# Expert 0's weight pieces later in the attention stage: three at the beginning, the others behind the second step

## The chip, the cores and the metric

One core of one Trainium2 chip runs the whole program. The metric is the device time of one execution, in microseconds. The kernel before took 2313.67 us (median of three runs, 2310.92 to 2315.62).

The engines are named as in the profile: PE is TensorE's matmul, PEld its weight load, DVE is VectorE, ACT is ScalarE, POOL is GpSimd, SP is SyncE, which issues the DMAs. Each works through its own queue in order.

## The reference

Three computations follow one another, all in float32. A decay attention over 4 batches of 8 heads, 768 positions of width 48; a mixture over 8 experts of all 3072 tokens, with gate weights balanced by eight rounds of normalization; a bilinear layer.

```python
f = 1.0 / (1.0 + np.exp(-f_logit))
for t in range(S):
    state = f[:, :, t, :, None] * state + np.einsum('bhd,bhe->bhde', k[:, :, t], v[:, :, t])
    y[:, :, t] = np.einsum('bhd,bhde->bhe', q[:, :, t], state)
...
P = np.exp(logits)                      # logits = x @ w_gate, less their maximum
for _ in range(8):
    P /= P.sum(1, keepdims=True) + 1e-09
    P /= P.sum(0, keepdims=True) + 1e-09
    P *= N / E
for e in range(E):
    h = np.maximum(x @ w1[e], 0.0)
    out += P[:, e:e + 1] * (h @ w2[e])
...
return (x @ w_a) * (x @ w_b) @ w_out
```

## The kernel before

The program has two parts with a plan of instructions each. The first holds attention, the first half of the normalization rounds, all of expert 0, and preparations for the second. The second holds experts 1 to 7 and the bilinear layer; the change leaves its rules alone.

Attention goes in 24 steps of 128 positions (`attention(s)`, lines 362 to 595): a step loads f, q, k and v, transposes them on TensorE, computes decays on ScalarE and VectorE (lines 395 to 413), forms scaled copies of q and k (419 to 460), masked products (m0, m8, m16, m32, lines 435 to 500), the state, and y (line 576). Its x goes through a DMA that rearranges it (line 584, tile xf), is split into a high and a low part (lines 593, 594), and is also stored (line 589). Products in this kernel use three matmuls: high by high, high by low, low by high.

Expert 0 (`expert0(b)`, line 612) works on pairs of steps as "fill": the planner gives its matmuls a share of TensorE's time beside attention. Its first product is with wi0 and wi1 (4 blocks each of h, line 624), its second with wo0 and wo1 (line 642). The splits of h are GpSimd's (line 631).

Expert 0's weights are prepared in 14 pieces (`add_piece`, line 243): for each half u three pieces wi of 128 x 512 and four wo of 128 x 384. A piece is loaded into one of two buffers raw (line 250; a piece of wi is two DMAs), copied to its high part by ScalarE (line 233), and GpSimd subtracts that from the raw value for the low part (line 235). A buffer is free for the next piece when GpSimd is done. The main stage's first weight preparation (`w1_prep(plan, 1000 * 12, 0)`, line 775) loads 128 x 256 blocks into the tile stage (line 731), forms five differences on GpSimd, copies them on ScalarE and subtracts on GpSimd; as instructions of the plan these have line 778 in the profile.

What sets the order is a list scheduler (`Plan.order`, line 82). It keeps a modelled time for each engine, and at each turn takes, of the operations whose dependencies are done on that engine, the one with the lowest priority number. An operation with a low number comes early, but one with a high number is taken too as soon as its engine has nothing better. Dependencies are keys, strings that an operation reads or writes in the plan. The planner's times only choose the order; on the chip, an instruction waits for the tiles that it really reads or writes.

Of the kernel before, what the change touches and what calls it, by code (L numbers as in the profile page):

```python
# [40 lines left out]
def f32(ap):  # L41
    return ap.bitcast(F32)
# [90 lines left out]
def kernel(  # L133
# [22 lines left out]
    KD = DM // 128  # L156
# [5 lines left out]
    FU = 512  # L162
    FT = FU // 128
# [4 lines left out]
    LATE = 4.0  # L168
# [27 lines left out]
    wd = [spill.tile(list(sh), F32, name=f"wd{n}") for n, sh in enumerate(  # L196
        ((DM, DFF2), (DM, DFF2), (DFF2, DM)))] if wide else [w_a, w_b, w_out]
# [28 lines left out]
    def take_raw(m):  # L226
        n = count["raw"] % len(raws)
        count["raw"] += 1
        return f"raw{n}", raws[n][:, :m]

    def split_ops(plan, prio, got, gk, hj, lj, key, m):

        plan.add(prio, "ACT", .11 + m * .00107, [gk], [key], lambda: nc.scalar.activation(  # L233
            out=hj, in_=got, func=AF.Copy))
        plan.add(prio + 1, "POOL", .1 + m * .0026, [gk, key], [key], lambda: nc.gpsimd.tensor_tensor(  # L235
            out=lj, in0=got, in1=f32(hj), op=ALU.subtract))

    def moe_rows(e, c, m):

        src = w1[e, :, c:c + m].rearrange(ROWS, **ROWS_N)  # L240
        return [[(64 * hd, 64, src[kk, hd]) for hd in range(2)] for kk in range(KD)]

    def add_piece(plan, prio, key, parts, hj, lj, reads=()):

        m = hj.shape[-1]
        rk, raw = take_raw(m)

        def get():
            for p0, n, src in parts:
                nc.sync.dma_start(out=raw[p0:p0 + n], in_=src.bitcast(I32))  # L250

        plan.add(prio, "SP", .05 + m * .0013, reads, [rk], get, LATE)
        split_ops(plan, prio + 9, f32(raw), rk, hj, lj, key, m)
# [73 lines left out]
    PE, DVE, ACT, POOL, SP = "PE", "DVE", "ACT", "POOL", "SP"  # L327
    plan = Plan()
    used = {"T": 0, "O": 0, "M": 0}

    def gate():
# [8 lines left out]
        out=wgs[:, :, E:], in0=wg, in1=f32(wgs[:, :, 0:E]), op=ALU.subtract))  # L340
# [256 lines left out]
    def logits(s, prio):  # L597
        xH, xL = (x[:, :, (s % 2) * 128:(s % 2) * 128 + 128] for x in b_x[(s // 2) % 2])

        def lg(ps):  # L600
            n = 2 * KD
            for i in range(n):
                a, m = ((xH, 2 * E), (xL, E))[i % 2]
                nc.tensor.matmul(
                    out=ps[:, :m], lhsT=a[:, i // 2, :], rhs=wgs[:, i // 2, :m], start=(i == 0), stop=(i == n - 1))

        kl, psl = take("O", p_O)
        plan.add(prio, PE, .54, [f"x{s % 4}", "wgs"], [kl], lambda: lg(psl))
        plan.add(prio, DVE, .08, [kl], [f"lg{s}"], lambda: nc.vector.tensor_reduce(
            out=logit[:, s, :], in_=psl[:, :2 * E].rearrange("p (two e) -> p e two", two=2), axis=AX.X, op=ALU.add))  # L610
# [36 lines left out]
            op(SP, .55, [ky], [], lambda ys=ys, tt=tt: nc.sync.dma_start(  # L647
                out=y0[b * (EB // 128) + tt], in_=ys), 3.0)

    for u in range(2):  # L650
        (ih, il), (oh, ol) = w_e0[u]
        rows = moe_rows(0, u * FU, FU)
        for n in range(KD):
            add_piece(plan, 1000 + 120 * (7 * u + n), f"e0i{u}{n}", rows[n], ih[:, n], il[:, n])
        for n in range(FT):
            f0 = u * FU + n * 128
            add_piece(plan, 1000 + 120 * (7 * u + KD + n), f"e0o{u}{n}", [(0, 128, w2[0, f0:f0 + 128, :])],
                      oh[:, n], ol[:, n])

    def sinkhorn(plan, prio, lo, hi, nm, bufs):  # L660

# [37 lines left out]

    for i in range(NSTEP):  # L700
        attention(i)
        if i:
            logits(i - 1, 1000 * i + 500)
        if i % 2 == 1:
            expert0(i // 2)
    logits(NSTEP - 1, 1000 * NSTEP)
    sinkhorn(plan, 1000 * NSTEP, 0, ROUNDS1, "T", p_T)
    phases = [("moe", 0), ("moe", 1), ("out", 0), ("moe", 2), ("out", 1), ("out", 2)]
# [10 lines left out]
    def w1_prep(plan, prio, n):  # L719

        ph, _, _, e, c = jobs[n]
        if phases[ph][0] == "moe":
            parts = moe_rows(e, c, PW)
        else:
            parts = [[(0, 128, wd[e][kk * 128:kk * 128 + 128, c:c + PW])] for kk in range(KD)]
        j = n % 2
        st, (wh, wl) = stage[j], w1s[j]
        for kk, slot in W_RAW:
            def get(kk=kk, slot=slot):
                for p0, m, src in parts[kk]:  # L730
                    nc.sync.dma_start(out=st[p0:p0 + m, slot:slot + 2, :].rearrange("p s f -> p (s f)"), in_=src)

            plan.add(prio, SP, .38, [] if phases[ph][0] == "moe" else [f"wd{e}"], [f"sg{j}{kk}"], get, LATE)
        sk = [f"sg{j}{kk}" for kk in range(KD)]
        for o, a, b in W_SUMS:
            plan.add(prio + 1, POOL, .5, sk, [f"sg{j}s"], partial(
                nc.gpsimd.tensor_tensor, out=st[:, o], in0=st[:, a], in1=st[:, b], op=ALU.subtract))
        for x in range(2):
            s = slice(5 * x, 5 * x + 5)
            key = f"w1{n % 2}{x}"  # L740
            plan.add(prio + 600, ACT, .74, sk + [f"sg{j}s"], [key], partial(
                nc.scalar.activation, out=wh[:, s], in_=st[:, s], func=AF.Copy))
            plan.add(prio + 601, POOL, 1.75, sk + [f"sg{j}s", key], [key], partial(
                nc.gpsimd.tensor_tensor, out=wl[:, s], in0=st[:, s], in1=f32(wh[:, s]), op=ALU.subtract))
# [21 lines left out]
    prio = 1000 * 12  # L766
    ab = [(f"xr{n}", b_xr[n]) for n in range(2)]
    for blk, z, i in ((1, 0, 0), (3, 1, 2), (None, 0, 1), (0, 0, 4), (4, 0, 8), (1, 1, None), (4, 0, 6), (0, 0, 5),
# [4 lines left out]
        if i is not None:  # L773
            x_sum(plan, prio, i, ab if len(X_OF[i]) > 1 else [], ab[z], POOL)
    w1_prep(plan, 1000 * 12, 0)
    with tc.manual_schedule():
        for fn in plan.order(SHARE):
# [7 lines left out]
    plan = Plan()  # L785
# [149 lines left out]
    if wide:  # L935
        for n, (r, c, m) in enumerate(((DM, DFF2, 256), (DM, DFF2, 256), (DFF2, DM, 192))):
            later += [(n, r0, c0, m) for c0 in range(0, c, m) for r0 in range(0, r, 128)]
    w1_prep(plan, -2000, 1)
    hs, ws = [], []
    for n, (ph, u, f, e, c) in enumerate(jobs):  # L940
# [37 lines left out]
        if n + 2 < len(jobs):  # L978
            w1_prep(plan, 1000 * (n + 1) - 500, n + 2)
# [48 lines left out]
```

## Time and profile before

| | |
|---|---|
| median of 3 runs | 2313.67 us |
| profiled execution | 2310.98 us |
| span of its trace | 2309.2 us |
| PE busy | 2235.4 us (97%) |
| DVE busy | 1457.6 us (63%) |
| ACT busy | 1045.5 us (45%) |
| POOL busy | 1089.9 us (47%) |

The shares are means over the whole program. The first part, with attention, lies within the first 495 us; the rows further below cut it in two stages. "Busy" of an engine is the time in which it had an instruction at work, stretched instructions included.

### The profile page before, as it was taken

To read this page: it belongs to the slowest core of one execution; us is meant where nothing else is said; L and a number is where in the kernel's file an instruction comes from. 1 tells how busy PE (TensorE), PEld (TensorE's weight loads), DVE (VectorE), ACT (ScalarE), POOL (GpSimd) and SP (SyncE) were. 2 spreads that over 40 slices of the span, in tenths; PEclk is the share of its full clock that TensorE was granted. 3 is DMA by queue.
4 is the path that set the end of the run, shared out by engine and by line. 5 is a ranking of instruction groups with operands and counts; after the bars stand their busy time and mean duration, and the time that the engine had idled before them with its cause. 6 is when DMAs were issued, how large, how long until landed. Compare 5 with 4: busy or idle time off the path is not lost.

```text
span 2309.2 us, 41089 instructions
## 1 busy us (share of the span) xinstructions
PE 2235.4 (97%) x15523; PEld 2010.4 (87%) x15523; DVE 1457.6 (63%) x2572; ACT 1045.5 (45%) x1988; POOL 1089.9 (47%) x1231
## 2 busy tenths in 40 slices
PE   5998999999999999999999999999999999999999
PEld 4887888888999999889999998888999999988888
DVE  7889787657766775576666544565444444455644
ACT  3555555535434444534434444554434444444442
POOL 4113212147544445554545456665444444475661
PEclk9999999999999999999999999999999999999999
DMA  6445433233232332332222223123111111221210
GB/s 125 104 94 117 97 84 83 51 113 85 82 93 86 85 89 70 108 90 81 76 78 76 56 64 94 48 76 103 43 54 50 54 49 42 82 76 44 80 49 28
DMA packets 278263, 176.67 MB, mean 77 GB/s; under 512 B 146608, under 2 KB 267696, under 8 KB 278064
## 3 DMA queue, kind: packets, MB, share of 16 engines
q1 hardware_dynamic: 278064, 174.04, 28.4%
q8 instruction: 122, 2.00, 0.4%
q14 instruction: 77, 0.63, 0.1%
HBM read 143.27 MB, written 25.95 MB: 73 GB/s over the span
## 4 chain that ended last, share of the span: by engine, by line
PE 79%; DVE 14%; ACT 2%; SPq 2%; issue 1%; DMA 1%; POOL 0%; DVEq 0%; ACTq 0%; POOLq 0%
PE pF L845 37%; PE pR L275 35%; PE pM L275 2%; PE pM L263 2%; DVE fi L413 2%; DVE z L987 2%; DVE gl L987 2%; DVE X L470 1%; SPq L584 1%; DMA xf<-q 1%; PE pO L569 1%; DVE X L519 1%; DVE fi L407 1%; DVE fi L405 1%; DVE q L456 1%
## 5 line engine op out<-in xcount | busy, mean ns | idle before, releaser
L275 PE MATMUL pR<-w2h,gl 128*128 128x384 f32 x1632 | 550.4, 337 | 5.4 <-DVE gl L987 5.4
L275 PE MATMUL pR<-w2l,gh 128*128 128x384 f32 x1632 | 551.1, 338 | 0.0
L275 PE MATMUL pR<-w2h,gh 128*128 128x384 f32 x1632 | 547.9, 336 | 0.6 <-DVE sk_c L693 0.6
L987 POOL TENSOR_TENSOR w1l<-stage,w1h 128x640 fp32r<-128x640 f32 x238 | 386.4, 1626 | 328.9 <-ACT w1h L987 317.2
L845 PE MATMUL pF<-xsh,w1h 128*128 128x512 f32 x1320 | 516.6, 391 | 10.1 <-ACT z L987 5.1
L845 PE MATMUL pF<-xsh,w1l 128*128 128x512 f32 x1320 | 523.7, 397 | 1.4 <-POOL w1l L987 1.4
L845 PE MATMUL pF<-xsl,w1h 128*128 128x512 f32 x1320 | 521.8, 395 | 0.0
L987 DVE TENSOR_TENSOR z<-pF,z 128x512 f32<-128x512 f32 x378 | 259.9, 689 | 356.8 <-PE pF L845 317.0
L987 POOL TENSOR_TENSOR stage<-stage 128x128 f32<-128x128 f32 x595 | 298.6, 517 | 376.9 <-DMA stage<-in_moe_w_dram 318.4
L987 ACT ACTIVATE gh<-z 128x512 fp32r<-128x512 f32 x324 | 203.9, 631 | 395.3 <-DVE z L987 388.9
L987 ACT ACTIVATE z<-pF 128x512 f32<-128x512 f32 x378 | 225.3, 597 | 294.0 <-PE pF L845 283.6
L275 PEld LDWEIGHTS pR<-w2l,gh 128*128 128x128 f32 x1632 | 306.1, 188 | 31.4
L275 PEld LDWEIGHTS pR<-w2h,gh 128*128 128x128 f32 x1632 | 306.6, 188 | 30.6 <-DVE sk_c L693 0.9
L987 DVE SCALAR_TENSOR_TENSOR acc<-pR,prob,acc 128x384 f32<-128x384 f32 x336 | 206.2, 614 | 201.0 <-PE pR L275 200.0
L275 PEld LDWEIGHTS pR<-w2h,gl 128*128 128x128 f32 x1632 | 306.4, 188 | 7.9 <-DVE gl L987 7.9
L845 PEld LDWEIGHTS pF<-xsh,w1l 128*128 128x128 f32 x1320 | 247.6, 188 | 55.0 <-POOL w1l L987 1.9
L845 PEld LDWEIGHTS pF<-xsh,w1h 128*128 128x128 f32 x1320 | 248.1, 188 | 46.1 <-ACT z L987 10.1
L235 POOL TENSOR_TENSOR w2l<-raw,w2h 128x384 fp32r<-128x384 f32 x204 | 233.7, 1156 | 99.4 <-ACT w2h L233 99.0
L845 PEld LDWEIGHTS pF<-xsl,w1h 128*128 128x128 f32 x1320 | 247.7, 188 | 28.8
L987 DVE SCALAR_TENSOR_TENSOR gl<-z,gh 128x512 fp32r<-128x512 f32 x252 | 221.5, 881 | 46.6 <-ACT gh L987 45.6
L987 ACT ACTIVATE w1h<-stage 128x640 fp32r<-128x640 f32 x238 | 174.3, 734 | 117.8 <-PE pF L845 97.2
L631 POOL TENSOR_TENSOR hl<-hf,hh 128x256 fp32r<-128x256 f32 x96 | 77.9, 814 | 263.6 <-ACT hf L629 240.7
(158 smaller groups left out, 2688.8 us busy)
## 6 DMA issues: line engine op xcount, KB each, us to landing
raw<-in_moe_w_dram SPq DMA_DIRECT2D x176, 192.0 KB, 2.5
stage<-in_moe_w_dram SPq DMA_DIRECT2D x504, 64.0 KB, 2.2
stage<-wd SPq DMA_DIRECT2D x108, 128.0 KB, 2.2
raw<-wd SPq DMA_DIRECT2D x36, 192.0 KB, 2.4
xr<-x1d SPq DMA_DIRECT2D x21, 256.0 KB, 3.7
nat_f<-in_f_logit_dram SPq DMA_DIRECT2D x24, 192.0 KB, 3.2
nat_q<-in_q_dram SPq DMA_DIRECT2D x24, 192.0 KB, 4.0
nat_k<-in_k_dram SPq DMA_DIRECT2D x24, 192.0 KB, 4.0
```

The source lines that it names most:

```text
L235: plan.add(prio + 1, "POOL", .1 + m * .0026, [gk, key], [key], lambda: nc.gpsimd.tensor_tensor(out=lj, in0=got, in1=f32(hj), op=ALU.subtract))
L263: nc.tensor.matmul(out=ps, lhsT=a[:, kk, fs], rhs=b[:, kk, :], start=(i == 0), stop=(i == 3 * KD - 1),)
L275: nc.tensor.matmul(out=ps, lhsT=a[:, off:off + 128], rhs=b, start=(start and i == 0), stop=(stop and i == n - 1))
L405: op(DVE, .6, ["e", f"fi0{z}"], [f"fi1{z}"], lambda: nc.vector.tensor_tensor(out=fi[:, 1], in0=e, in1=fi[:, 0], op=ALU.mult))
L407: op(DVE, .6, ["e"], [f"fi1{z}"], lambda: nc.vector.scalar_tensor_tensor(out=fi[:, 1], in0=fi[:, 1], scalar=2.0, in1=e, op0=ALU.subtract, ...
L413: op(DVE, .34, [], [f"fi0{z}", f"fi1{z}"], lambda a=a, c=c: nc.vector.tensor_tensor(out=fi[:, :, :, a], in0=fi[:, :, :, a], in1=fi[:, :, : ...
L456: op(DVE, .34, [f"g{n}{z}"], [f"q3{z}"], lambda: nc.vector.tensor_tensor(out=qv[:, :, 1, :], in0=qv[:, :, 1, :], in1=bc(g[:, :, 0], n), op ...
L470: nc.vector.copy_predicated(X[r, hd].rearrange("j g (b two e) -> j g b two e", two=2, e=n)[:, :, :, 1, :], mbc(r, o, nb, n), A1[r, lv].rea ...
L519: op(DVE, .34, [f"q3{z}", f"g32{z}"], [f"Xq{z}"], lambda hd=hd, r=r: nc.vector.tensor_tensor(out=X[r, hd, :, 32:64], in0=pct(q3)[r, :, 32: ...
L631: op(POOL, .64, [f"hh{ft}", kf], [f"hl{ft}"], lambda hh=hh, hl=hl, hf=hf: nc.gpsimd.tensor_tensor(out=hl, in0=hf, in1=f32(hh), op=ALU.subt ...
L845: nc.tensor.matmul(out=ps, lhsT=a[:, slot], rhs=b, start=(new and i == 0), stop=(i == 3 * len(prods) - 1), skip_group_check=not new)
L987: fn()
```

## The change

The pieces of expert 0's weights are no longer added in one loop with priorities from 1000 on. The three pieces of wi0 are added within step 0 with priority 3.5, between its loads of k and v. The three pieces of wi1 and the eight of wo get "Xa1" as a key that they read, the masked products of step 1, and priorities from 2000 and 2100 on. The three blocks that the main stage's first preparation loads get "xd00" as a key that they read, which the stores of x of the first eight steps write.

```diff
@@ -647,15 +647,14 @@
             op(SP, .55, [ky], [], lambda ys=ys, tt=tt: nc.sync.dma_start(
                 out=y0[b * (EB // 128) + tt], in_=ys), 3.0)
 
-    for u in range(2):
+    def e0_weights(prio, u, after):
         (ih, il), (oh, ol) = w_e0[u]
         rows = moe_rows(0, u * FU, FU)
         for n in range(KD):
-            add_piece(plan, 1000 + 120 * (7 * u + n), f"e0i{u}{n}", rows[n], ih[:, n], il[:, n])
-        for n in range(FT):
-            f0 = u * FU + n * 128
-            add_piece(plan, 1000 + 120 * (7 * u + KD + n), f"e0o{u}{n}", [(0, 128, w2[0, f0:f0 + 128, :])],
-                      oh[:, n], ol[:, n])
+            add_piece(plan, prio + n / 8, f"e0i{u}{n}", rows[n], ih[:, n], il[:, n], after)
+        return [partial(add_piece, plan, 2100 + 500 * u + 100 * n, f"e0o{u}{n}",
+                        [(0, 128, w2[0, u * FU + n * 128:u * FU + n * 128 + 128, :])], oh[:, n], ol[:, n])
+                for n in range(FT)]
 
     def sinkhorn(plan, prio, lo, hi, nm, bufs):
 
@@ -699,6 +698,13 @@
 
     for i in range(NSTEP):
         attention(i)
+
+        if i == 0:
+            rest = e0_weights(3.5, 0, [])
+        if i == 1:
+            rest += e0_weights(2000, 1, ["Xa1"])
+            for get in rest:
+                get(["Xa1"])
         if i:
             logits(i - 1, 1000 * i + 500)
         if i % 2 == 1:
@@ -730,7 +736,7 @@
                 for p0, m, src in parts[kk]:
                     nc.sync.dma_start(out=st[p0:p0 + m, slot:slot + 2, :].rearrange("p s f -> p (s f)"), in_=src)
 
-            plan.add(prio, SP, .38, [] if phases[ph][0] == "moe" else [f"wd{e}"], [f"sg{j}{kk}"], get, LATE)
+            plan.add(prio, SP, .38, [f"wd{e}"] if phases[ph][0] == "out" else [] if n else ["xd00"], [f"sg{j}{kk}"], get, LATE)
         sk = [f"sg{j}{kk}" for kk in range(KD)]
         for o, a, b in W_SUMS:
             plan.add(prio + 1, POOL, .5, sk, [f"sg{j}s"], partial(
```

SyncE at the beginning, before: `raw` is a buffer of a weight piece, `nat`, `vn` and `Y` are attention's loads, `wg` the gate's weights.

```order
L377 DMA vn_122<-in_v_dram 128x8x48
L382 DMA Y_124<-in_v_dram 64x4x48
L336 DMA mask<-in_mask_dram 128x128
L250 DMA raw_108<-in_moe_w_dram 64x1x512 x2
L375 DMA nat_f_117<-in_f_logit_dram 128x8x48
L375 DMA nat_q_119<-in_q_dram 128x8x48
L375 DMA nat_k_121<-in_k_dram 128x8x48
L382 DMA Y_124<-in_v_dram 64x4x48
L377 DMA vn_123<-in_v_dram 128x8x48
L382 DMA Y_125<-in_v_dram 64x4x48
L334 DMA wg<-in_moe_w_gate_dram 64x1x8 x6
```

And in the changed kernel, from the second piece on (the first, raw_108, stands right ahead of these rows):

```order
L250 DMA raw_109<-in_moe_w_dram 64x1x512 x2
L377 DMA vn_122<-in_v_dram 128x8x48
L382 DMA Y_124<-in_v_dram 64x4x48
L336 DMA mask<-in_mask_dram 128x128
L375 DMA nat_f_117<-in_f_logit_dram 128x8x48
L375 DMA nat_q_119<-in_q_dram 128x8x48
L375 DMA nat_k_121<-in_k_dram 128x8x48
L377 DMA vn_123<-in_v_dram 128x8x48
L382 DMA Y_124<-in_v_dram 64x4x48
L250 DMA raw_108<-in_moe_w_dram 64x1x512 x2
L382 DMA Y_125<-in_v_dram 64x4x48
L334 DMA wg<-in_moe_w_gate_dram 64x1x8 x6
```

The first two pieces of wi0 stand ahead of the loads of v, the third ahead of wg: six DMAs of weights are issued ahead of wg where two were.

SyncE around the first rearranging of x (line 584, tile xf_138, step 0), before:

```order
L250 DMA raw_109<-in_moe_w_dram 128x384
L250 DMA raw_108<-in_moe_w_dram 128x384
L375 DMA nat_q_118<-in_q_dram 128x8x48
L375 DMA nat_k_120<-in_k_dram 128x8x48
L250 DMA raw_109<-in_moe_w_dram 64x1x512 x2
L377 DMA vn_122<-in_v_dram 128x8x48
L250 DMA raw_108<-in_moe_w_dram 64x1x512 x2
L382 DMA Y_124<-in_v_dram 64x4x48
L250 DMA raw_109<-in_moe_w_dram 64x1x512 x2
L584 DMA xf_138<-q_133 64x1x128 x6
L250 DMA raw_108<-in_moe_w_dram 128x384
```

And in the changed kernel:

```order
L375 DMA nat_q_118<-in_q_dram 128x8x48
L375 DMA nat_k_120<-in_k_dram 128x8x48
L377 DMA vn_122<-in_v_dram 128x8x48
L382 DMA Y_124<-in_v_dram 64x4x48
L584 DMA xf_138<-q_133 64x1x128 x6
L250 DMA raw_109<-in_moe_w_dram 64x1x512 x2
L250 DMA raw_108<-in_moe_w_dram 64x1x512 x2
L382 DMA Y_124<-in_v_dram 64x4x48
L375 DMA nat_f_117<-in_f_logit_dram 128x8x48
L589 DMA x1d<-xf_138 128x3x128
L377 DMA vn_123<-in_v_dram 128x8x48
L382 DMA Y_124<-in_v_dram 64x4x48
```

The weight pieces that stood in front of it stand behind it.

GpSimd from the first split on, before: `wi0l` and the like are low parts of expert 0's weights, `stage` and `w1l` belong to the main stage's preparation.

```order
L235 TENSOR_TENSOR wi0l<-raw_108,wi0h 128x512
L235 TENSOR_TENSOR wi0l<-raw_109,wi0h 128x512
L235 TENSOR_TENSOR wi0l<-raw_108,wi0h 128x512
L778 TENSOR_TENSOR stage_93<-stage_93 128x128 x3
L235 TENSOR_TENSOR wo0l<-raw_109,wo0h 128x384
L778 TENSOR_TENSOR stage_93<-stage_93 128x128 x2
L235 TENSOR_TENSOR wo0l<-raw_108,wo0h 128x384
L778 TENSOR_TENSOR w1l_92<-stage_93,w1h_91 128x640 x2
L235 TENSOR_TENSOR wo0l<-raw_109,wo0h 128x384
L235 TENSOR_TENSOR wo0l<-raw_108,wo0h 128x384
L235 TENSOR_TENSOR wi1l<-raw_109,wi1h 128x512
L235 TENSOR_TENSOR wi1l<-raw_108,wi1h 128x512
```

And in the changed kernel, where `hl` are the splits of expert 0's h:

```order
L235 TENSOR_TENSOR wi0l<-raw_108,wi0h 128x512
L235 TENSOR_TENSOR wi0l<-raw_109,wi0h 128x512
L235 TENSOR_TENSOR wi0l<-raw_108,wi0h 128x512
L235 TENSOR_TENSOR wi1l<-raw_109,wi1h 128x512
L235 TENSOR_TENSOR wi1l<-raw_108,wi1h 128x512
L235 TENSOR_TENSOR wi1l<-raw_109,wi1h 128x512
L235 TENSOR_TENSOR wo0l<-raw_108,wo0h 128x384
L631 TENSOR_TENSOR hl_173<-hf_181,hh_165 128x256
L235 TENSOR_TENSOR wo0l<-raw_109,wo0h 128x384
L631 TENSOR_TENSOR hl_174<-hf_182,hh_166 128x256
L235 TENSOR_TENSOR wo0l<-raw_108,wo0h 128x384
L631 TENSOR_TENSOR hl_175<-hf_181,hh_167 128x256
```

The eleven later pieces begin with wi1, the last seven stand among the splits of h, and the preparation of the main stage is gone from here.

## Rows read from the trace of the kernel before

**Rows 1.** Stages: length, busy us (instructions) by engine, clock, DMA share, GB/s

```profile
core 0: us, PE busy (x) PEld busy (x) DVE busy (x) ACT busy (x) POOL busy (x), PEclk, DMA share, GB/s
20.00:73.00 53.00, 35.19 (x528) 30.32 (x527) 49.13 (x96) 24.85 (x56) 20.51 (x19) 1.00 0.61 133
73.00:440.00 367.00, 342.58 (x5429) 311.94 (x5430) 311.78 (x694) 204.99 (x519) 85.65 (x99) 1.00 0.42 90
```

**Rows 2.** Tile pM from 60 to 130: durations in ns, first and last start

```profile
L263 PE MATMUL pM<-xH,wi0h x24: 277/283/580, 72.9 to 122.2; 128*128 128x256 f32 x24
...
L275 PE MATMUL pM<-wo0h,hh x8: 334/378/446, 93.0 to 106.2; 128*128 128x384 f32 x8
```

**Rows 3.** VectorE from 20 to 73 by line and shape: busy us, mean ns

```profile
L413 DVE TENSOR_TENSOR fi<-fi 112x256 f32<-112x256 f32 x9 | 7.3, 812 | 0.2
...
L405 DVE TENSOR_TENSOR fi<-e,fi 112x512 f32<-112x512 f32 x3 | 3.6, 1211 | 1.8 <-ACT e L400 1.7
...
L458 DVE TENSOR_TENSOR k<-k,g 112x256 f32<-112x256 f32 x6 | 3.5, 590 | 0.0
...
L456 DVE TENSOR_TENSOR q<-q,g 112x256 f32<-112x256 f32 x6 | 3.1, 514 | 0.0
...
L407 DVE SCALAR_TENSOR_TENSOR fi<-fi,e 112x512 f32<-112x512 f32 x3 | 2.8, 917 | 0.1
...
L504 DVE TENSOR_TENSOR k<-k,g 112x256 f32<-112x256 f32 x3 | 2.3, 752 | 0.1
...
L397 DVE TENSOR_SCALAR fi<-e 112x512 f32<-112x512 f32 x3 | 2.1, 708 | 0.9 <-ACT e L395 0.9
...
L460 DVE TENSOR_TENSOR g<-g 112x16 f32<-112x16 f32 x3 | 1.5, 484 | 0.0
```

**Rows 4.** Timeline of VectorE: start us, us, instruction, idle before it

```profile
6.33 0.43 DVE L397 TENSOR_SCALAR fi<-e 112x512 f32<-112x512 f32 x1 [6.33 <-ACT e L395]
...
8.11 0.69 DVE L405 TENSOR_TENSOR fi<-e,fi 112x512 f32<-112x512 f32 x1 [1.36 <-ACT e L400]
...
16.94 0.18 DVE L338 CAST wgs<-wg 128x24 fp32r<-128x24 f32 x1 [1.82 <-DMA wg<-in_moe_w_gate_dram]
...
17.04 0.16 DVE L460 TENSOR_TENSOR g<-g 112x16 f32<-112x16 f32 x1
...
20.25 1.36 DVE L405 TENSOR_TENSOR fi<-e,fi 112x512 f32<-112x512 f32 x1 [1.73 <-ACT e L400]
...
23.19 0.41 DVE L458 TENSOR_TENSOR k<-k,g 112x256 f32<-112x256 f32 x1
...
57.62 0.69 DVE L437 TENSOR_TENSOR q<-bq,fi 112x512 f32<-112x512 f32 x1 [0.96 <-DMA xf<-q]
...
62.12 0.62 DVE L413 TENSOR_TENSOR fi<-fi 112x256 f32<-112x256 f32 x1
```

**Rows 5.** GpSimd from 0 to 75 by line and shape: busy us, mean ns

```profile
L235 POOL TENSOR_TENSOR wo1l<-raw,wo1h 128x384 fp32r<-128x384 f32 x4 | 4.5, 1138 | 12.9 <-ACT wo1h L233 12.9
...
L235 POOL TENSOR_TENSOR wo0l<-raw,wo0h 128x384 fp32r<-128x384 f32 x4 | 4.3, 1084 | 4.2 <-ACT wo0h L233 4.2
...
L235 POOL TENSOR_TENSOR wi1l<-raw,wi1h 128x512 fp32r<-128x512 f32 x3 | 3.9, 1315 | 8.4 <-ACT wi1h L233 5.0 <-DMA raw<-in_moe_w_dram 3.3
...
L778 POOL TENSOR_TENSOR w1l<-stage,w1h 128x640 fp32r<-128x640 f32 x2 | 3.2, 1634 | 0.5 <-ACT w1h L778 0.5
...
L778 POOL TENSOR_TENSOR stage<-stage 128x128 f32<-128x128 f32 x5 | 3.2, 645 | 5.4 <-DMA stage<-in_moe_w_dram 5.2
```

**Rows 6.** Timeline of SyncE: the gate's weights

```profile
11.62 3.79 SPq L334 DMA_DIRECT2D wg<-in_moe_w_gate_dram  x6
```

**Rows 7.** Timeline of TensorE: one group of four transposes

```profile
69.97 1.10 PE L390 MATMUL pT<-ident,nat_k 128*112 128x128 f32 x4
```

**Rows 8.** Timeline of GpSimd: two pieces of expert 0

```profile
39.74 1.31 POOL L235 TENSOR_TENSOR wo0l<-raw,wo0h 128x384 fp32r<-128x384 f32 x1 [0.84 <-ACT wo0h L233]
...
73.76 1.46 POOL L235 TENSOR_TENSOR wo1l<-raw,wo1h 128x384 fp32r<-128x384 f32 x1 [5.91 <-ACT wo1h L233]
```

**Rows 9.** Waits of TensorE from 75 to 440: us in total, times, longest

```profile
PE pO L509 <- DVE k L504: 10.2, 10, 2.6
...
PE pO L569 <- DVE S L558: 0.4, 1, 0.4
```

## The prediction

> **What bounds the kernel now.** I read the table of stages first. From 73 to 440 us TensorE is busy 342.6 of 367 us: there it is the limit, with 24.4 us lost. From 20 to 73 us it is busy only 35.2 of 53 us, and VectorE 49.1 of 53 [rows 1]: attention's first three steps run alone, expert 0 has no x yet, and VectorE sets the pace. So the question is when expert 0's first matmul can start (72.9 us [rows 2]), how much TensorE has done by then, and what happens to the stalls of the long stage behind it.
>
> What slows VectorE before 73 us is seen in the groups of its instructions beside single ones of the same shape. L405 takes 1211 ns on average in the stretch and 0.69 us when nothing else runs, L458 590 ns against 0.41 us, L460 484 ns against 0.16 us [rows 3, 4]. Eight groups, each as its busy time less its count times the undisturbed duration: L413 7.3 - 9 x 0.62 = 1.7; L405 3.6 - 3 x 0.69 = 1.5; L407 2.8 - 3 x 0.69 = 0.7; L458 3.5 - 6 x 0.41 = 1.0; L456 3.1 - 6 x 0.41 = 0.6; L504 2.3 - 3 x 0.41 = 1.1; L397 2.1 - 3 x 0.43 = 0.8; L460 1.5 - 3 x 0.16 = 1.0. Together 8.5 us, while GpSimd was busy for 20.5 us [rows 1] with the splits of weights [rows 5]: 0.42 us of VectorE lost for each microsecond of GpSimd work.
>
> **The change part by part.** Nothing is added or removed: the 14 pieces, each two copies and one DMA or two, and the first preparation of the main stage keep their instructions. They change places. "Xa1" and "xd00" are keys of the planner alone, the DMAs do not read those tiles, so no semaphore wait is added; only the order in each queue moves.
>
> *Before expert 0 starts.* Of GpSimd's work that stood in the stretch, what is left there by the new order is the three wi1 pieces and one of wo0: 3 x 1.315 + 1.084 = 5.0 us [rows 5] (wi0's third piece runs before 20 us, in a stretch where VectorE waits anyway). At 0.42 that costs VectorE 2.1 us instead of 8.5, so 6.4 us less.
>
> SyncE's queue takes something back. Four more DMA issues now stand ahead of the six of the gate's weights; at 3.79 / 6 = 0.63 us each [rows 6] they come 2.5 us later, and with them the CAST of wgs, which VectorE waits for at 16.94 [rows 4] and now would start at 19.4. Behind it the order of VectorE is as it was. Part is regained: the wait of 1.73 us in front of L405 at 20.25 [rows 4] came from a weight copy that stood in ScalarE's queue ahead of the exponential and waited for its DMA; in the new order that copy has its data by then. Loss between 0.8 and 2.5 us; I take 1.2, since the exponential of step 1 still follows L397, which is late. Two copies ahead of step 0's chain cost up to one of their durations, which the wait for wgs hides; without that cover it would be 0.6 us.
>
> One gain lies in the queue: raw DMAs stood ahead of the six that store x of step 0, and VectorE waited 0.96 us for these at 57.62 [rows 4]. The new order has them behind: +0.9.
>
> So expert 0 starts 6.4 - 1.2 + 0.9 = 6.1 us earlier, at about 66.8 us. One transpose group of four (1.10 us [rows 7]) that ran before it now comes after, so of the 6.1 us TensorE gains 5.0 in idle time.
>
> *After expert 0 starts.* The rest comes later: three wo0 and four wo1 pieces, 3 x 1.084 + 4 x 1.138 = 7.8 us, of which one was there before (73.76 us [rows 8], 1.1 without its own disturbance), and the main stage's first preparation, 3.2 + 3.2 = 6.4 us [rows 5], now among the sums of x. Together 13.1 us more GpSimd work in the stage from 73 to 440. The ends for it: nothing, if other TensorE work covers each delay, and 13.1 x 0.42 = 5.5 us, if each reaches TensorE. In that stage TensorE waited 15.7 us for VectorE (five rows of the waits, the first 10.2 us and the last 0.4 [rows 9]) beside 85.65 us of GpSimd [rows 1]: 15.7 / 85.65 = 0.18 for each, if all of it came from there. That is the nearest row, and I take 13.1 x 0.18 = 2.4 us.
>
> One rule of the Trainium skill speaks against the change. The rows show two-input instructions of VectorE stretched while GpSimd splits. The page "SBUF — State Buffer", section "Who interferes with whom", says that a VectorE instruction with two SBUF inputs and a GpSimd one that reads SBUF exclude each other, and the later one blocks until the other is done. By that the stall goes wherever the split goes, and could be as long as the split itself: 13.1 us instead of 5.5 for the moved work if all of it were on the path. The trace agrees on who is stretched, and gives 0.42 instead of 1 for the share.
>
> *At nothing.* The ready time of main-stage weights: their reader is the first matmul behind 495 us, and they are issued behind the eighth step. The stage behind 495 us keeps its order. The order between 73 and 440 is drawn anew by the planner at many places; I put 0 for that and widen the range by 3 us on each side.
>
> **The sum.** 5.0 - 2.4 = 2.6 us. The profiled execution took 2310.98 us in a span of 2309.2, 2.7 us under the median of 2313.67, so 2308.4 for such an execution, and 2311.1 beside the median. That is 0.11%; about 0.2%, or 4.6 us, is what a measurement of this kernel can tell from none.
>
> **The rivals.**
>
> *The moved work is hidden altogether.* For it: ScalarE and GpSimd have room from 73 us on (205 and 86 of 367 us [rows 1]), and VectorE idles there for 55 us. Against: TensorE takes its instructions in order, so a late VectorE does reach it, as the waits show. The full 5.0 us stay, perhaps with a better drawn order: 2308.7, reaching to 2306.
>
> *Slower: expert 0's own weights come late.* Each piece needs one of two raw buffers, so the next DMA waits in SyncE's queue for GpSimd, which now has expert 0's splits of h between the pieces; and the stores of x stand behind those DMAs. Before, the eight steps from the piece at 39.74 to the one at 73.76 us took 34.0 us [rows 8], 4.25 each. The first moved piece can follow the store of x: about 57.6 - 6.1 + 2.5 = 54 us. At that pace the eleventh starts at 54 + 10 x 4.25 = 96.5 and is ready at 97.6. Expert 0 asks for wo0 at 66.8 + (93.0 - 72.9) = 86.9 [rows 2], and for the last of wo1 some 7 us behind that (an estimate), at 94. If the pace stays as it was, TensorE stands still for about 4 us at wo1; it decides once a piece takes over 3.9 us. Against: what slowed the pace before were waits behind attention's loads, and six pieces have the queue nearly to themselves. With every stretch reaching TensorE as well: 5.0 - 5.5 - 4 = -4.5, so 2318.2. By the skill's rule at its full length it would be 7.6 us more.
>
> *The start does not come earlier.* The late wgs, or a load that now comes behind, holds VectorE as long as the splits did. Against: VectorE's wait for loads before 73 us is small apart from wgs. It would give 2313.67 + 2.4 = 2316.1.
>
> **How the numbers follow.** Forecast 0.50, all hidden 0.30, slower by late weights 0.12, no earlier start 0.08. The forecast's own range is 2307.5 to 2315. For all cases 2304.5 to 2317.5. Faster by over 0.2%: 0.8 of the hidden case and 0.25 of the forecast, 0.37. Slower by over 0.2%: half of the late-weights case, a quarter of no earlier start and 0.1 of the forecast, 0.13. Within it: 0.50.
>
> **What would show it.** Right: in the stages, GpSimd falls from 20.5 to about 5 to 8 us before expert 0, the groups of [rows 3] shrink to their undisturbed durations, the CAST of wgs starts near 19.4, the first matmul of expert 0 near 67 us. Behind it TensorE's idle time up to 440 us would go from 24.4 to about 27. Wrong: a first matmul at 70 us or later; a wait of TensorE for wo1 (late weights); or a stage behind it whose idle time moves by more than the start gains, up or down, which would put the cause in the newly drawn order.

## The result and the profile after

The changed kernel took 2330.18 us (median of five runs, 2327.45 to 2332.16); the kernel before, run beside it, 2314.54. The ratio is 1.0071, with a 95% interval of 1.0058 to 1.0083: 15.6 us slower, where the forecast was 2311.1 and its range ended at 2317.5. The profiled execution of the changed kernel took 2329.62 us in a span of 2327.8.

The part before expert 0 came nearly as forecast. Stages of the changed kernel, cut where its expert 0 starts, in the columns of [rows 1]:

```profile
core 0: us, PE busy (x) PEld busy (x) DVE busy (x) ACT busy (x) POOL busy (x), PEclk, DMA share, GB/s
20.00:67.00 47.00, 34.95 (x528) 30.51 (x528) 43.42 (x98) 20.67 (x47) 5.70 (x4) 1.00 0.52 104
67.00:440.00 373.00, 338.17 (x5238) 309.54 (x5234) 304.07 (x673) 202.17 (x505) 95.62 (x106) 0.95 0.43 92
```

Tile pM of the changed kernel, durations in ns, first and last start:

```profile
L263 PE MATMUL pM<-xH,wi0h x24: 278/400/580, 67.3 to 123.5; 128*128 128x256 f32 x24
...
L275 PE MATMUL pM<-wo0h,hh x8: 334/334/421, 86.2 to 90.0; 128*128 128x384 f32 x8
```

Expert 0 starts at 67.3 us instead of 72.9 [rows 2]; 66.8 was expected. GpSimd has 5.7 us of work before it (20.5 in [rows 1]; 5 to 8 expected). The instructions of VectorE in that stretch, as in [rows 3]:

```profile
L413 DVE TENSOR_TENSOR fi<-fi 112x256 f32<-112x256 f32 x9 | 5.6, 619 | 0.2
...
L456 DVE TENSOR_TENSOR q<-q,g 112x256 f32<-112x256 f32 x6 | 3.6, 601 | 0.0
...
L560 DVE TENSOR_TENSOR S<-S,g 112x192 f32<-112x192 f32 x4 | 2.5, 632 | 0.0
L458 DVE TENSOR_TENSOR k<-k,g 112x256 f32<-112x256 f32 x6 | 2.5, 412 | 0.0
L519 DVE TENSOR_TENSOR X<-q,g 64x256 f32<-64x256 f32 x3 | 2.3, 772 | 0.0
...
L405 DVE TENSOR_TENSOR fi<-e,fi 112x512 f32<-112x512 f32 x3 | 2.1, 685 | 0.6 <-ACT e L400 0.6
L407 DVE SCALAR_TENSOR_TENSOR fi<-fi,e 112x512 f32<-112x512 f32 x3 | 2.0, 682 | 0.0
...
L504 DVE TENSOR_TENSOR k<-k,g 112x256 f32<-112x256 f32 x3 | 1.3, 425 | 0.1
L397 DVE TENSOR_SCALAR fi<-e 112x512 f32<-112x512 f32 x3 | 1.3, 423 | 0.9 <-ACT e L395 0.9
...
L460 DVE TENSOR_TENSOR g<-g 112x16 f32<-112x16 f32 x3 | 0.5, 174 | 0.0
```

L405 is down from 1211 to 685 ns, L504 from 752 to 425, L460 from 484 to 174. By the same sum as in the prediction the eight groups are now stretched by 1.2 us and not 8.5. L560 and L519 were not among the eight; they took 353 and 409 ns on average before, and are now stretched by 1.1 us each. Together that is 3.4 us, where 2.1 was forecast. Single instructions of VectorE, start and length:

```profile
19.34 0.18 DVE L338 CAST wgs<-wg 128x24 fp32r<-128x24 f32 x1 [2.75 <-DMA wg<-in_moe_w_gate_dram]
...
21.50 0.69 DVE L405 TENSOR_TENSOR fi<-e,fi 112x512 f32<-112x512 f32 x1 [0.58 <-ACT e L400]
...
52.84 1.45 DVE L560 TENSOR_TENSOR S<-S,g 112x192 f32<-112x192 f32 x1
54.22 1.50 DVE L456 TENSOR_TENSOR q<-q,g 112x256 f32<-112x256 f32 x1
...
60.52 1.50 DVE L519 TENSOR_TENSOR X<-q,g 64x256 f32<-64x256 f32 x1
```

The CAST of wgs came at 19.34 (19.4 expected) and held L405 of step 1 until 21.50 (20.25 in [rows 4]). The last three rows are long where GpSimd is at work. Its timeline:

```profile
52.25 3.19 POOL L235 TENSOR_TENSOR wi1l<-raw,wi1h 128x512 fp32r<-128x512 f32 x2 [33.37 <-ACT wi1h L233]
60.39 1.36 POOL L235 TENSOR_TENSOR wi1l<-raw,wi1h 128x512 fp32r<-128x512 f32 x1 [4.95 <-ACT wi1h L233]
```

L456 at 54.22 took 1.50 us for 0.41 undisturbed and ended at 55.72, the second split of the pair at 55.44. So it lost 1.09 us beside a split of 1.42, and ended 0.28 us behind it. The rule of the Trainium skill ("SBUF — State Buffer", section "Who interferes with whom": the later of the two blocks until the earlier is done) agrees with these single rows. Over the stretch VectorE lost 3.4 us beside 5.7 us of GpSimd work, 0.6 for each: more than the 0.42 that the prediction took as a mean, and less than the whole.

Behind 67 us it went wrong. The waits of TensorE in that stage, in the columns of [rows 9]:

```profile
PE pO L509 <- DVE k L504: 9.7, 8, 2.6
PE pA L497 <- DVE k L458: 5.1, 4, 2.2
PE pA L484 <- DVE k L458: 4.6, 3, 1.9
PE pA L433 <- DVE X L477: 4.5, 1, 4.5
...
PE pT L390 <- ACT e L395: 2.6, 1, 2.6
```

Two rows are new: 4.5 us for the masked copy L477 and 2.6 us for L395, once each. From the first matmul of expert 0 to the first of the main stage, the stage of the kernel before and then of the one after (columns as in the first fence):

```profile
72.90:495.00 422.10, 397.68 (x5976) 365.06 (x5975) 332.39 (x755) 227.05 (x577) 99.01 (x117) 1.00 0.38 83
```

```profile
core 0: us, PE busy (x) PEld busy (x) DVE busy (x) ACT busy (x) POOL busy (x), PEclk, DMA share, GB/s
67.30:512.80 445.50, 409.26 (x5980) 378.23 (x5979) 333.21 (x755) 232.15 (x585) 113.50 (x130) 0.96 0.38 83
```

The stretch is 445.5 us long and was 422.1, so 23.4 longer. TensorE idles 36.2 us of it and 24.4 before (+11.8), and for the same work it is busy 11.6 us longer, at a granted clock of 0.96 instead of 1.00 (of its two levels, 1.2 and 2.4 GHz, more of the lower). Less the 5.6 us of the earlier start, the main stage begins 17.8 us later (512.8 for 495.0). From there on nothing changed: 1815.0 us to the end of the span, 1814.2 before. (That makes 18.6 us between the two profiled executions; between the medians it is 15.6.)

Where the stage goes wrong first is seen in the copies L477 of VectorE. Before, step 2 has them at 53.5 and step 3 at 75.8 and 77.3 us; after, step 3's come at 93.67:

```profile
53.49 1.48 DVE L477 COPY_PREDICATED X<-mask,pA 64x512 f32<-64x512 int32 x2 [0.20 <-PE pA L433]
...
75.80 0.76 DVE L477 COPY_PREDICATED X<-mask,pA 64x512 f32<-64x512 int32 x1
...
77.26 0.74 DVE L477 COPY_PREDICATED X<-mask,pA 64x512 f32<-64x512 int32 x1
```

```profile
93.67 1.48 DVE L477 COPY_PREDICATED X<-mask,pA 64x512 f32<-64x512 int32 x2
```

TensorE of the changed kernel meanwhile:

```profile
86.25 0.42 PE L275 MATMUL pM<-wo0h,hh 128*128 128x384 f32 x1
...
90.34 0.34 PE L275 MATMUL pM<-wo0h,hl 128*128 128x384 f32 x1
95.21 1.59 PE L433 MATMUL pA<-bq,bk 48*64 48x64 f32 x32 [4.53 <-DVE X L477]
96.73 0.69 PE L275 MATMUL pM<-wo1h,hh 128*128 128x384 f32 x1
...
112.92 1.06 PE L497 MATMUL pA<-q,k 48*32 48x32 f32 x32 [2.22 <-DVE k L458]
114.64 1.10 PE L390 MATMUL pT<-ident,nat_q 128*112 128x128 f32 x4 [0.66 <-ACT bk L423]
...
115.76 0.41 PE L263 MATMUL pM<-xL,wi0h 128*128 128x256 f32 x1
```

The 24 matmuls of wo0 stand in one lump, with nothing of attention between them (from 86.25 to 90.34; before, the first and the last of them are 13 us apart [rows 2]). Then TensorE waits 4.53 us for the late copies. By 105 us expert 0's matmuls are used up, TensorE has attention alone and waits for VectorE, and when expert 0 starts again the same matmul of 128 x 256 takes 0.41 us where it took 0.28. From 90 to 120 us, before and then after:

```profile
90.00:120.00 30.00, 28.62 (x470) 26.04 (x467) 27.45 (x67) 17.90 (x44) 3.67 (x6) 1.00 0.49 103
```

```profile
90.00:120.00 30.00, 22.50 (x333) 20.35 (x333) 23.68 (x55) 10.53 (x28) 2.38 (x3) 0.83 0.39 84
```

TensorE does 333 matmuls where it did 470, and the clock is 0.83.

What held the copies back lies in the planner's bookkeeping. A weight DMA that names "Xa1" in its reads is entered as a *reader* of that tile. The next operation that writes the key, step 3's first copy L477, then gets a dependency on all eleven loads, as if they had to be done with the tile. No semaphore comes of it. But the planner places the copies only when its model has issued the last load (at 84.95 us of its own time instead of 62.3), and everything that hangs on them moves back too.

### The profile page after: what moved, and what is told of

It is laid out like the page before. It is cut to its first block, busy times and chain, and to the rows that moved or that the text cites. A ratio compares the mean times of both kernels' runs of the same rounds, so it can differ in the third digit from the quotient of the medians.

```text
span 2327.8 us, 41092 instructions
## 1 busy us (share of the span) xinstructions
PE 2246.7 (97%) x15523; PEld 2024.8 (87%) x15523; DVE 1449.5 (62%) x2572; ACT 1046.1 (45%) x1988; POOL 1091.7 (47%) x1231
## 4 chain that ended last, share of the span: by engine, by line
PE 80%; DVE 12%; ACT 3%; SPq 2%; DMA 2%; issue 1%; DVEq 0%; ACTq 0%
PE pF L851 36%; PE pR L275 35%; PE pM L263 3%; PE pM L275 2%; DVE z L993 2%; DVE gl L993 1%; DVE fi L413 1%; SPq L584 1%; DVE X L470 1%; DVE X L477 1%; DMA xf<-q 1%; PE pO L569 1%; PE pA L445 1%; DVE X L519 1%; DVE fi L407 0%
```

## The experiments

Most kernels here take the plan's list of operations and change its order alone, by

```diff
-        for fn in plan.order(SHARE):
-            fn()
+        for t in SEQ.split():        # an order written out
+            plan.ops[at[t]][4]()
```

so that the moved work and the redrawn order can be told apart. All results first: "e0" is the first matmul of expert 0, "main" the first of the main stage, "idle" and "clock" are TensorE's between the two, all from the one profiled execution of each. The clock column counts the time ahead of a trace's first clock record as 1.00, which moves it by less than 0.01 here.

| kernel | median | ratio to before, 95% | e0 | main | idle | clock |
|---|---|---|---|---|---|---|
| before | 2314.5 | | 72.9 | 495.0 | 24.4 | 1.00 |
| changed | 2330.2 | 1.0071 (1.0058 to 1.0083) | 67.3 | 512.8 | 36.2 | 0.96 |
| weights_only | 2333.2 | 1.0079 (1.0061 to 1.0097) | 69.9 | 514.9 | 36.5 | 0.96 |
| prep_only | 2329.8 | 1.0068 (1.0048 to 1.0088) | 72.5 | 516.5 | 33.3 | 0.96 |
| old_order_new_pieces | 2323.6 | 1.0044 (1.0029 to 1.0059) | 67.4 | 509.5 | 32.9 | 0.96 |
| new_order_old_pieces | 2333.1 | 1.0079 (1.0060 to 1.0098) | 75.7 | 516.4 | 35.7 | 0.97 |
| no_war | 2320.0 | 1.0026 (1.0014 to 1.0039) | 68.1 | 504.2 | 28.8 | 0.97 |
| old_order_new_pieces2 | 2316.5 | 1.0004 (0.9992 to 1.0016) | 67.4 | 500.6 | 27.7 | 0.98 |
| old_order_prep | 2315.6 | 1.0004 (0.9994 to 1.0013) | 71.1 | 498.5 | 24.9 | 0.98 |
| before_gap | 2315.0 | 1.0006 (0.9995 to 1.0017) | 73.1 | 498.0 | 25.8 | 0.99 |
| before_hold | 2331.2 | 1.0078 (1.0060 to 1.0097) | 72.3 | 515.8 | 32.1 | 0.95 |
| old_order_pieces | 2314.7 | 0.9999 (0.9989 to 1.0008) | 69.9 | 497.4 | 26.3 | 0.99 |
| n_gap19 | 2330.4 | 1.0071 (1.0056 to 1.0086) | 75.4 | 515.7 | 29.2 | 0.96 |
| n_turn9 | 2325.4 | 1.0053 (1.0035 to 1.0071) | 73.9 | 509.2 | 29.7 | 0.99 |
| after_then_old | 2329.5 | 1.0067 (1.0052 to 1.0082) | 67.7 | 511.2 | 32.2 | 0.95 |
| old_then_after | 2323.9 | 1.0043 (1.0027 to 1.0060) | 66.7 | 510.1 | 36.1 | 0.97 |
| gap_then_old | 2322.4 | 1.0040 (1.0025 to 1.0055) | 74.7 | 507.6 | 25.8 | 0.97 |
| old_then_gap | 2323.1 | 1.0041 (1.0026 to 1.0056) | 72.7 | 507.3 | 30.3 | 0.97 |

**weights_only.** The changed kernel with the preparation's line left as before.

```diff
-            plan.add(prio, SP, .38, [f"wd{e}"] if phases[ph][0] == "out" else [] if n else ["xd00"], [f"sg{j}{kk}"], get, LATE)
+            plan.add(prio, SP, .38, [] if phases[ph][0] == "moe" else [f"wd{e}"], [f"sg{j}{kk}"], get, LATE)
```

> The 14 weight pieces as in the changed kernel, the main stage's first preparation where it was before. Theory 'new order' (the planner's newly drawn order lets TensorE run out of expert 0's matmuls and wait for VectorE, and its clock falls): the order is drawn anew from 50 us on here too, so 2322 to 2336 us. Theory 'late pieces' (the splits among expert 0's own work stretch VectorE and hold the queue): the same, 2325 to 2332. Theory 'preparation' (its 13 moved GpSimd and ScalarE instructions hit the sums of x near 200 us): 2308 to 2316.

It lost as much as the whole change, so the preparation is not needed for the loss.

**prep_only.** The opposite: the kernel before with the change's line of the preparation.

> The weight pieces as before, only the main stage's first preparation behind the eighth step. Theory 'new order': the order changes from about 25 us on only as far as GpSimd and ScalarE make room, so anything from 2308 to 2325, with TensorE's idle time in the stretches where its order differs. Theory 'late pieces': 2309 to 2316. Theory 'preparation': 2322 to 2332.

It lost as much again. Each half has the whole loss, and the two do not add. The theory of the new order had put this kernel at 2325 at most; that was a miss. Here no operation that stayed in place got a new dependency.

**old_order_new_pieces.** Moved pieces and preparation, all else in the order of before.

> All instructions but the 14 pieces and the preparation stand in the order of the kernel before; these two stand where the changed kernel has them (behind the same instruction of their engine, or ahead of their first reader). Theory 'new order': the start gains as forecast and nothing is lost behind it, 2306 to 2313 us. Theory 'late pieces': the loss stays, 2322 to 2332. Theory 'preparation': 2320 to 2330.

The order's theory missed too (2306 to 2313), and 2323.6 fits the other two. But there was a fault in my merge: it still honoured the false dependency, and six pieces stood in GpSimd's queue ahead of expert 0's own splits. One row of TensorE's waits from 60 to 130 us shows it (lines of this kernel are shifted by 114: L743 is the activation hf):

```profile
PE pM L377 <- ACT hf L743: 6.9, 1, 6.9
```

**new_order_old_pieces.** The changed kernel's order, with pieces and preparation where before has them.

> The reverse: all instructions but the 14 pieces and the preparation stand in the order of the changed kernel, these where the kernel before has them. Theory 'new order': the loss is here, and the start's gain is not, 2328 to 2342 us. Theories 'late pieces' and 'preparation': 2310 to 2318.

The whole loss without any moved work. The theories of late pieces and of the preparation fall here: neither is needed for it.

**no_war.** The loads wait for the last writer of Xa1 and are not entered as readers.

```diff
-            w, r = self.last.setdefault(key, (None, []))
+            w, r = self.last.setdefault(key.lstrip("@"), (None, []))
...
-            r.append(n)
+            r.extend([n] if key[0] != "@" else [])
...
-            rest += e0_weights(2000, 1, ["Xa1"])
+            rest += e0_weights(2000, 1, ["@Xa1"])
```

> The changed kernel, but the eleven later weight pieces wait for Xa1's last writer without being entered as its readers, so that in the planner's model step 3's first masked copy no longer waits for their loads; the order is drawn anew once more. If that one false dependency causes the loss: TensorE's 4.5 us wait at the first L433 behind wo0 is gone, the main stage's first matmul stands at 490 to 497, and the time is 2306 to 2314. If any redrawn order costs about as much as this one: first main-stage matmul at 505 to 517 and 2322 to 2335. If the moved pieces themselves cost it (VectorE beside POOL at 60 to 100 us): the same 2322 to 2335, and the next kernel is slow too.

Between the two theories: from 1.0071 to 1.0026, intervals apart. Without the false dependency 10 of the 15.6 us are gone; 6 stay. TensorE no longer waits for L477, and from 90 to 120 us it does 417 matmuls instead of 333:

```profile
90.00:120.00 30.00, 26.99 (x417) 24.16 (x411) 27.81 (x65) 15.07 (x37) 4.20 (x7) 0.94 0.52 111
```

This order is drawn anew as well, so how much of the 10 us is the dependency's own is not shown.

**old_order_new_pieces2.** As the first of its name, without the false dependency in the merge.

> Every instruction stands in the order of the kernel before, except the fourteen weight pieces and the first preparation, which stand on SP, ScalarE and POOL where the changed kernel has them; the pieces no longer stand ahead of the splits of the hidden activations in POOL's queue, as six of them did in the first kernel of this kind. If the redrawn order causes the loss: expert 0's first matmul at 66 to 69, the main stage's first matmul at 488 to 495, and 2306 to 2313. If the moved pieces themselves cost it, where they now stand: first main-stage matmul at 505 to 515 and 2320 to 2332.

Between the two theories again. No loss is left beyond what can be measured, but no gain either: the start's 5.5 us are in the profile (67.4) and gone at 500.6.

**old_order_prep.** The preparation alone at its new place, in the old order.

> Every instruction stands in the order of the kernel before, the fourteen weight pieces too; only the first preparation (its loads, additions and splits) stands where the changed kernel has it, about 200 us. If the redrawn order causes the loss: within 4 us of the kernel before, 2311 to 2318. If POOL's and VectorE's collision at 200 us costs it: 2322 to 2332, and PE busy time in 200 to 280 down from 72 to about 68.

As the order's theory had it; the same move in a redrawn order (prep_only) cost 14 us more. Stages of this kernel, and of the kernel before:

```profile
40.00:60.00 20.00, 15.09 (x245) 13.30 (x241) 16.66 (x36) 11.14 (x26) 6.08 (x5) 0.50 0.46 106
200.00:280.00 80.00, 71.66 (x1055) 64.70 (x1053) 60.54 (x128) 41.71 (x106) 32.01 (x31) 0.94 0.48 106
```

```profile
40.00:60.00 20.00, 14.63 (x250) 12.91 (x246) 17.03 (x38) 10.19 (x24) 6.02 (x5) 1.00 0.36 87
200.00:280.00 80.00, 72.31 (x1113) 65.55 (x1112) 64.74 (x138) 44.72 (x111) 25.29 (x28) 1.00 0.47 103
```

From 200 to 280 us GpSimd has 32 us of work for 25 and TensorE loses 0.7 us of busy time, not 4.

**before_gap.** Nothing moved; `GAP = 0.2` became `0.21`.

> The kernel before with no work moved, only the planner's estimate of a hand-over between engines at 0.21 us for 0.20; its order is drawn anew from somewhere in the first stage on. If redrawn orders cost what this change cost whatever they are for: 2320 to 2335. If a redrawn order is worth a few us to either side, as the prediction had it: 2308 to 2318.

No difference. But in the traces the order of TensorE's instructions first differs at 307 us, two thirds through attention, so it says nothing of a redraw near expert 0's start. The next two do.

**before_hold.** Nothing moved; one operation of the plan, step 3's first copy, gets an earliest time.

```diff
-        left, users, ready_at = [], [[] for _ in self.ops], [0.0] * len(self.ops)
+        left, users, ready_at = [], [[] for _ in self.ops], [84.95 * (n == 344) for n in range(len(self.ops))]
```

> The kernel before, no weight piece and no preparation moved; in the planner's model alone, step 3's first masked copy (L477) may not start before 84.95 us, which is when the changed kernel's plan lets it start (before's own plan: 62.3). If that false dependency causes most of the loss: 8 to 14 us slower, 2322 to 2330, with a run dry of TensorE between 90 and 120 us. If the dependency matters only together with the moved pieces: 2311 to 2318.

The whole loss, 16 us, above the 8 to 14 expected. VectorE's copies, and the stretch from 90 to 120 us:

```profile
53.37 1.49 DVE L477 COPY_PREDICATED X<-mask,pA 64x512 f32<-64x512 int32 x2 [0.21 <-PE pA L433]
...
95.58 1.52 DVE L477 COPY_PREDICATED X<-mask,pA 64x512 f32<-64x512 int32 x2
```

```profile
90.00:120.00 30.00, 26.22 (x355) 24.17 (x354) 20.79 (x49) 11.15 (x27) 0.76 (x1) 0.77 0.40 88
```

They come at 95.58, as in the changed kernel (93.67), TensorE does 355 matmuls for 470, and the clock is 0.77. So holding that one step back in the plan is enough for a loss of this size; n_gap19 below has one without it. The run dry that I expected was not one long wait but a lack of work for 30 us.

**old_order_pieces.** The fourteen pieces at their new places; all else, the preparation too, in the old order.

> Every instruction, the first preparation too, stands in the order of the kernel before; only the fourteen weight pieces stand where the changed kernel has them. With the preparation moved as well this gave 2316.5, with the preparation alone 2315.6. If the earlier start is worth anything at the end: 2307 to 2312, and faster than both kernels. If the gain is eaten inside the first stage whatever the preparation does (what ends it is not the start): 2313 to 2318, the main stage's first matmul at 494 to 499 with expert 0's first at 66 to 69.

No gain: 0.9999 (0.9989 to 1.0008). Expert 0 starts at 69.9; with the preparation moved as well it was 67.4.

**n_gap19.** `GAP = 0.19`, nothing moved.

> The kernel before with the planner's hand-over between engines at 0.19 us for 0.20, nothing moved on purpose; its order differs from the 54th TensorE instruction on, that is before expert 0 begins. If any early redraw of the order costs what the preparation's alone cost (14 us in the kernel with it alone): 2322 to 2335. If redraws without a held-back step scatter by a few us: 2311 to 2320.

16 us lost with step 3's copies where they were (75.92 us). The longest waits of TensorE from 66 to 500 us, and its stage from expert 0 on:

```profile
PE pA L484 <- DVE k L458: 16.7, 9, 3.9
```

```profile
75.40:515.70 440.30, 411.12 (x5980) 378.32 (x5979) 330.35 (x755) 226.03 (x577) 101.06 (x117) 0.96 0.37 79
```

Here L484 waits 16.7 us for L458, 1.8 in the kernel before. But other waits are shorter: in the stage of the second row TensorE idles 4.8 us longer than before and is busy 13.4 us longer, at a clock of 0.96. Another place and mostly another form, the same price.

**n_turn9.** `TURN = 0.09` for `0.08`, nothing moved.

> The kernel before with the planner's cost of a change from attention to experts at 0.09 us for 0.08, nothing moved on purpose; its order differs from the 151st TensorE instruction on, within expert 0. If early redraws cost: 2322 to 2335. If they scatter by a few us: 2311 to 2320.

11 us lost. A few us to either side, as the prediction had it, is wrong for a redraw that begins this early.

**after_then_old, old_then_after.** The two orders spliced at 125 us of the planner's time.

> All of the changed kernel's moves. The planned order is spliced: up to 125 us of the planner's time (about 135 us on the chip) it is the changed kernel's, with step 3's copies held back; behind that everything stands in the relative order of the kernel before. The same moves in the old order throughout gave 2316.5, in the changed order throughout 2330.2. If the loss is made where the copies are held back: 2324 to 2333. If the order behind it makes the loss: 2314 to 2320. If each does half: 2321 to 2325.

> The opposite splice of the same two orders: up to 125 us of the planner's time the order of the kernel before (with the pieces where the changed kernel has them), behind that the changed kernel's order. If the loss is made where the copies are held back: 2312 to 2319. If the order behind it makes the loss: 2324 to 2333. If each does half: 2321 to 2325.

The first has the whole loss: what is drawn up to 125 us makes it, also with the old order behind. The second should then have had none, and has 0.43%. The parts do not add up to 0.71%.

**gap_then_old, old_then_gap.** The same splices of n_gap19's order with the old one.

> Nothing moved on purpose. Up to 125 us of the planner's time the order of the kernel with 0.19 us for a hand-over (2330.4 by itself), behind that the relative order of the kernel before. If an early redraw is what costs: 2324 to 2333. If the order behind it does: 2311 to 2318.

> The opposite splice: up to 125 us of the planner's time the order of the kernel before, behind that the order drawn with 0.19 us. If an early redraw is what costs: 2311 to 2318. If the order behind it does: 2324 to 2333.

Neither theory: each half costs 0.4%. From expert 0's first matmul to the main stage's, gap_then_old:

```profile
74.70:507.60 432.90, 407.15 (x5980) 372.84 (x5979) 332.91 (x755) 226.47 (x577) 102.22 (x117) 0.97 0.38 81
```

It idles hardly longer than the kernel before (25.8 us for 24.4), yet takes 432.9 us for 422.1: nearly all of its loss in this execution is busy time, 407.2 us for 397.7, at a granted clock of 0.97.

## Why the prediction was wrong

- *The start:* right. 67.3 us for 66.8; TensorE's idle time before it fell from 28.3 to 24.0 us, 4.3 for 5.0. The term for VectorE was small, 3.4 us of stretching instead of 2.1 beside the GpSimd work that stayed.
- *"No semaphore wait is added; only the order in each queue moves":* true of the chip, and yet the error starts here. I asked what the loads wait for, and not who waits for the loads in the plan.
- *The later work, 2.4 us:* probably too small. In the old order with all moves (old_order_new_pieces2) the stretch from expert 0 to the main stage took 433.2 us, 11.1 more than before, over the upper end of 5.5; 3.3 of it is idle time and the rest busy time at a lower clock. Some 4.7 of the 11.1 lie in which executions were profiled: this kernel's is 1.1 us above its median, that of the kernel before 3.6 below. By its ratio (1.0004, so 0.9 us lost, and by the interval from 1.9 gained to 3.7 lost) it is about 6: the 5.0 that the start was to give, and 0.9 more. This eats the start's gain, and the forecast of a small gain would have been no change.
- *"The order between 73 and 440 is drawn anew by the planner at many places; I put 0 for that and widen the range by 3 us on each side":* the step that failed. With the same moves the redrawn order costs 2330.2 - 2316.5 = 13.7 us, or 15.5 by the two ratios. One way into it is shown: the false dependency holds step 3's copies back, and holding them back alone costs as much (before_hold). It is not the only way, since prep_only and n_gap19 lose as much with nothing held back. The planner's own model, in which the step could have been seen, shows some of these losses and not others. Worked through off the chip, `Plan.order` ends the first part at 445.2 us of its own time for the kernel before, 452.9 for the changed one, 450.0 for before_hold and 455.0 for n_turn9, but at 444.6 for prep_only, 445.0 for n_gap19 and 445.3 for no_war.
- *The rivals:* the slower one had the sign, by luck: its 4 us at wo1 look like the 4.53 us that TensorE waited just ahead of its first wo1 matmul (96.73), but that wait was for attention's copies (the last split of wo1, from 93.79 to 94.80 us, was done by then), and the rival priced the whole at 2318.2. No earlier start, and the hidden case: no.
- *The main stage at nothing:* right, within 0.8 us.
- *What would show it wrong:* idle time up to 440 us should have gone to about 27 and went to 34.8 (373 less 338.17). That sign, put down to a newly drawn order, was the right one.

What stays open: why the order of before is the better one. Eleven orders that leave it before 145 us (twelve kernels, without the faulty merge) lost 0.26 to 0.79%, four of them with nothing moved and no step held, two of these spliced; none gained. The five kernels with the step held lost 0.67 to 0.79%, the seven others 0.26 to 0.71%. The loss comes sometimes as waits, sometimes as busy time at a lower clock, at different places. The parts of the changed kernel's do not add (0.67 and 0.43% for 0.71), those of n_gap19's nearly do (0.40 and 0.41 for 0.71). No kernel here beats the one before.

## What to carry to other kernels

In a planned kernel a key used only to place an operation also puts that operation ahead of the key's next writer: list who waits for the moved work in the plan, and depend on the last writer alone. Compare the planner's modelled end before and after: here that gave the held step away, though not every loss. A redrawn order is a cost of its own, and with an order that is better than its neighbours it is a loss, not zero with a spread. To price moved work apart from it, move the work within the written-out old order, and nudge a constant of the planner with nothing moved.

## What the runs showed of the hardware

From 40 to 60 us the profile gives a granted clock of 0.50 for old_order_prep and 1.00 for the kernel before, with nearly the same work (245 and 250 matmuls, 15.09 and 14.63 us busy; the rows above). One might read from that that the lower clock cost nothing. But the same matmuls took the same time in both, here one group of each, first the kernel before and then old_order_prep:

```profile
L390 PE MATMUL pT<-ident,nat_q 128*112 128x128 f32 x4 | 1.1, 430 | 0.0
```

```profile
L504 PE MATMUL pT<-ident,nat_q 128*112 128x128 f32 x4 | 1.1, 428 | 0.0
```

So TensorE ran at the same level in both, and the two rows tell nothing of what the clock costs there. The step to the upper level shows in the durations of one shape. In the changed kernel it comes with TensorE at work without a gap since 65.40 us:

```profile
71.10 0.41 PE L263 MATMUL pM<-xH,wi0l 128*128 128x256 f32 x1
...
72.07 0.28 PE L263 MATMUL pM<-xL,wi0h 128*128 128x256 f32 x1
```

The profile gives 1.00 from 67.3 to 71.8 us too, where each of these matmuls took 0.41 us or more. So a 1.00 ahead of the first step up is to be checked against durations. Behind expert 0's start, where TensorE is the limit, gap_then_old was busy 9.5 us longer than the kernel before at 0.97 for 1.00.
